# Loads of k and stores of the output with an outermost dimension of 32 or more rows, in a threshold-attention plus MLP kernel

## The chip, the cores and the metric

The kernel runs on one core of one Trainium2 chip. The metric is device time in microseconds (us), the median of several executions. Ratios use runs of the fast state alone; a median is taken over all runs of a kernel, and two of these (n2_order_only, v_late_weights) contain one slow run. The profile is one execution taken by the hardware profiler. PE is the TensorE matrix engine, DVE is VectorE, ACT is ScalarE, POOL is GpSimd, SP is SyncE, which here only issues DMAs. Times inside a profile count from the first instruction ("span").

## The reference

```python
# q, k, v: [8 batches, 8 heads, 576, 64] float32; tau = 0.02
scores = (q @ k.T) / 8
scores = where(scores >= max(scores, -1) - tau, scores, -1e9)
attn   = softmax(scores)                 # in each head
x      = (attn @ v), heads side by side  # [4608 tokens, 512]
h      = x @ w_in                        # w_in  [512, 2048]
out    = maximum(0.01 * h, h) @ w_out    # w_out [2048, 512], out [4608, 512] float32
```

## The kernel before

The program is built by a tile framework whose scheduler orders the instructions of each engine. It works in 160 steps: a step is one pair of heads and one chunk of 128 query rows (the fifth chunk has 64). A step computes scores on PE, takes their maximum on VectorE, exponentials on ScalarE, normalises on GpSimd, **turns the weights by a DMA transpose** (`wt<-w`), and five steps later (LAG) multiplies them with v on PE. Each batch's q and k are split into high and low fp16 parts and also turned by DMA transposes (`qst<-qs`, `kst<-ks`). Between these, PE works off units of the MLP; each 128 finished rows are stored.

All transposes, all q and k loads and all stores are issued from SP. v and the weights are loaded with a cast from GpSimd.

```python
    def load_qk(b, hb):                     # 4 heads: g = pair, h = head in the pair
        ...
        src_q = q[b, ds(4*hb, 4), :, :].rearrange("(g h) (p t) d -> h p g (t d)", h=2, t=9)
        src_k = k[b, ds(4*hb, 4), :, :].rearrange("(g h) (x p t) d -> x h p g (t d)", h=2, x=2, t=9)
        for g in range(2):
            for x in range(2):              # source [h=2, p=32, 576]: 64 rows of 2304 bytes
                nc.sync.dma_start(out=km[ds(64*x, 64), g, :], in_=src_k[x, :, :, g, :])
            if b == 0:
                nc.sync.dma_start(out=qm[:, g, :], in_=src_q[:, :, g, :])
        if b > 0:
            nc.sync.dma_start(out=qm[:, :, :], in_=src_q)
    ...
    def rows_of(b, c):                      # where 128 rows of the output go: [2, 64, 512]
        if c == 4:
            return out[ds(b*S, 2*S), :].rearrange("(b p t) d -> t b p d", t=9, b=2)[8]
        return out[ds(b*S, S), :].rearrange("(p t) d -> t p d", t=9)[ds(2*c, 2)]
    ...
            def fin():                      # the end of an MLP row block
                osb = sb.tile([128, 512], FP32, tag="osb", bufs=2, name="osb")
                nc.vector.tensor_copy(out=osb, in_=op)
                nc.sync.dma_start(out=G.stores[m], in_=osb)
    ...
            def evac():                     # attention output, PSUM -> x, fp16
                nc.scalar.activation(out=G.x[:, :, ds(col, n)], in_=pvp, func=AF.Copy, ...)
```

Of the kernel before, what the change touches and what calls it, by code (L numbers as in the profile page):

```python
# [12 lines left out]
AF = mybir.ActivationFunctionType  # L13
# [3 lines left out]
def kernel(  # L17
# [16 lines left out]
    nc = tc.nc  # L34
    B, H, S, D = q.shape
# [39 lines left out]
    def load_qk(b, hb):  # L75


        qm = sb.tile([128, 2, 576], FP32, tag="qm", bufs=2, name="qm")
        km = sb.tile([128, 2, 576], FP32, tag="km", bufs=2, name="km")
        src_q = q[b, ds(4 * hb, 4), :, :].rearrange("(g h) (p t) d -> h p g (t d)", h=2, t=9)  # L80
        src_k = k[b, ds(4 * hb, 4), :, :].rearrange("(g h) (x p t) d -> x h p g (t d)", h=2, x=2, t=9)
        for g in range(2):
            for x in range(2):
                nc.sync.dma_start(out=km[ds(64 * x, 64), g, :], in_=src_k[x, :, :, g, :])
            if b == 0:
                nc.sync.dma_start(out=qm[:, g, :], in_=src_q[:, :, g, :])
        if b > 0:
            nc.sync.dma_start(out=qm[:, :, :], in_=src_q)
        qms[b, hb], kms[b, hb] = qm, km

    def load_v(b):
# [106 lines left out]
    def h_unit(G, u):  # L198
        n = G.n
        per = 512 // n  # L200

        def mms():
            if u == 0:
                G.g = sb.tile([128, NJ, 256], FP16, tag="gT", bufs=2, name="gT")[:, :, 0:n]
            hp = ps.tile([128, per, n], FP32, tag="h", bufs=2, name="hp")
            for jj in range(per):
                j = u * per + jj
                for g in range(4):
                    nc.tensor.matmul(  # L209
                        out=hp[:, jj, :], lhsT=w_in16[:, g, ts(j, 128)], rhs=G.x[:, g, :],  # L210
                        start=(g == 0), stop=(g == 3), skip_group_check=True,
                    )

            def act():
                nc.scalar.activation(out=G.g[:, ds(u * per, per), :], in_=hp, func=AF.Relu, bias=0.0, scale=0.99)  # L215
                if (u + 1) * per == NJ:
                    for m in range(n // 128):
                        for c in range(4):
                            oq.append(lambda m=m, c=c: o_unit(G, m, c))
            return act  # L220
        return mms
# [47 lines left out]
    def rows_of(b, c):  # L269

        if c == 4:
            return out[ds(b * S, 2 * S), :].rearrange("(b p t) d -> t b p d", t=9, b=2)[8]
        return out[ds(b * S, S), :].rearrange("(p t) d -> t p d", t=9)[ds(2 * c, 2)]


    steps = []
# [9 lines left out]
    def group_of(b, c):  # L286

        if c == 4:
            key = ("t", b // 4)
            if key not in groups:  # L290
                t = b // 4
                groups[key] = Group(256, [rows_of(4 * t + 2 * m, 4) for m in range(2)])
            return groups[key], 64 * (b % 4), b % 4 == 3
        if b == B - 1 and c >= 2:
            if (b, c) not in groups:
                groups[b, c] = Group(128, [rows_of(b, c)])
            return groups[b, c], 0, True
        key = (b, c // 2, 0)
        if key not in groups:
            groups[key] = Group(256, [rows_of(b, 2 * (c // 2) + cc) for cc in range(2)])  # L300
        return groups[key], 128 * (c % 2), c % 2 == 1
# [41 lines left out]
    def pv(s):  # L343
        b, c, p = steps[s]
        wt = st[s]["wt"]
        vt = vts[b]
        n = 128 if c < 4 else 64
        if p == 0:
            pvt[0] = ps.tile([128, NP, n], FP32, tag="pv", bufs=1, name="pv")
        pvp = pvt[0]  # L350
        for j in range(5):
            for h in range(2):
                rhs = wt[:, 5 * h + j, :] if c < 4 else wt[:, j, ds(64 * h, 64)]
                nc.tensor.matmul(  # L354
                    out=pvp[ds(64 * h, 64), p, :], lhsT=vt[:, 2 * p + h, j, :], rhs=rhs,
                    start=(j == 0), stop=(j == 4), skip_group_check=True,
                    tile_position=(0, 64 * h),
                )
        if p == NP - 1:
            G, col, done = group_of(b, c)  # L360

            def evac():
                nc.scalar.activation(out=G.x[:, :, ds(col, n)], in_=pvp, func=AF.Copy, bias=0.0, scale=1.0)
                if done:
                    for u in range(NJ * G.n // 512):
                        hq.append(h_unit(G, u))
            return evac
        return None
# [30 lines left out]


    load_qk(0, 0)
    load_qk(0, 1)
    prep_q = deque()
    for p in range(NP):
# [9 lines left out]
    for g in range(4):  # L414
        nc.gpsimd.dma_start(
            out=w_out16[:, ds(4 * g, 4), :],
            in_=moe_w_out[ds(512 * g, 512), :].rearrange("(j p) d -> p j d", p=128))

    tick = {}
    for b in range(1, B):  # L420
        s0 = 20 * (b - 1)
        tick.setdefault(max(0, s0 - 4), []).append(lambda b=b: load_qk(b, 0))
        tick.setdefault(s0 + 12, []).append(lambda b=b: load_v(b))
        tick.setdefault(s0 + 4, []).append(lambda b=b: load_qk(b, 1))
        for p in range(NP):
            for i, t in enumerate(prep_tasks(b, p)):
                tick.setdefault(s0 + 1 + 4 * p + (i * 4) // 7, []).append(t)
# [7 lines left out]
    for s in range(NS + LAG + 1):  # L435
# [15 lines left out]
        if live:  # L451
            d = st[s]
# [19 lines left out]
        if live:  # L472
            nc.vector.scalar_tensor_tensor(  # L473
                out=d["W"][:, 0, 0:576], in0=s32, scalar=tb[:, 0:1], in1=E,
# [22 lines left out]
    while hq or oq:  # L497
        for q_ in (hq, oq):
            if q_:
                f = q_.popleft()()  # L500
# [37 lines left out]
```

## Time and profile before

| | before |
|---|---|
| median | 989.47 us (988.62 to 990.32, 2 runs) |
| PE busy, mean granted clock | 62%, 0.851 |
| first scores on PE | 55.9 us |
| step 10 starts its exp | 155.8 us |
| step 159 (the last) | 934.3 us |

The page first. The engine table (busy us, share of the span, number of instructions) and three rows of the 40 slices (tenths; PEclk is the granted PE clock, DMA the busy share of the 16 DMA engines), then the DMA queues:

```profile
PE 609.4 (62%) x4880; PEld 329.4 (33%) x4880; DVE 528.6 (54%) x1580; ACT 453.0 (46%) x894; POOL 440.1 (45%) x572
...
PEclk9999977777958876887679987888879998989998
DMA  3999989999979699998999999999996998849720
GB/s 82 101 139 89 129 158 178 114 140 128 145 90 142 97 117 96 136 139 116 126 100 138 116 140 104 113 126 130 127 144 79 150 136 118 120 78 115 102 60 33
...
q1 hardware_dynamic: 324768, 105.94, 87.3%
q0 software_dynamic: 23808, 8.92, 11.9%
```

No compute engine is full. DMA looks full, but moves little. What PE waits for (view of waits: who waited for whom, total us, times, longest us):

```profile
PE pv L354 <- DMA wt<-w: 124.3, 34, 10.3
PE sc L313 <- DMA qst<-qs: 109.3, 6, 55.9
PE sc L313 <- DVE s L377: 72.0, 28, 12.4
PE pv L354 <- ACT xT L363: 42.4, 15, 13.2
```

Two of the first three are transposes. The timeline shows one such case (start us, duration us, then, in brackets, the idle time before and what ended it). A pair of `qst` transposes occupies SP for 10.76 us and ScalarE stands 12.24 us for it; the next pair takes SP 3.57 us:

```profile
345.51 10.76 SPq L177 DMA_TRANSPOSE qst<-qs  x2
357.77 3.57 SPq L177 DMA_TRANSPOSE qst<-qs  x2
358.45 0.68 ACT L155 ACTIVATE qs<-qm 128x576 f16<-128x576 f32 x1 [12.24 <-DMA qst<-qs]
```

The trace also has every DMA packet: start, duration, size, queue. Sizes tell what a packet belongs to: 256 bytes on SP's queue are transposes, 2304 bytes are q and k rows, 2048 bytes are output rows. Counting them by the microsecond around that case (mean packets in flight, and packets completed):

```
us in span   transposes      q, k rows       output rows
             flight  done    flight  done    flight  done
  344          0.0      0      2.1     22      0.0      0     k load: 2 in flight
  347          0.0      0     16.6    147      0.0      0     q load: 16 in flight
  348          9.0    339      8.8     63      0.6      5
  349         20.0    112      0.2      2      1.9     21     a store begins: 2 in flight
  350 to 352  22.0      0      0.0      0      2.1     25     (each us) transposes stand
  353         22.0      0      0.3      3      1.8     22
  354         22.0      0      1.7     18      0.4      5     store ends, a k load begins
  356         20.3   1074      0.0      0      0.0      0     transposes run
```

Here is the whole case in eight lines (us 345 is like 344; 346 and 355, in which one state passes into the next, are left out). The store and the k load keep two packets in flight, as if only two of the 16 DMA engines worked. The transposes' packets are in flight all the while, so the DMA row shows 9 tenths, but not one completes for five microseconds; when the narrow transfers are over, a thousand complete in one.

### The profile page before, as it was taken

The numbers are of one execution on the slowest core, as the hardware profiler recorded it, in microseconds if no ns is written. First come the engines' busy times: TensorE is split into PE (matmuls) and PEld (weight loads), VectorE is DVE, ScalarE is ACT, GpSimd is POOL, SyncE is SP. The second block draws the span as 40 slices with busy tenths as digits, with TensorE's granted clock in tenths as the row PEclk, the third lists the DMA queues.
The fourth block names the chain that finished last, engine by engine and source line by source line (L and its number), as shares of the span: only waits on it lengthen the run. The fifth ranks groups of instructions, "written<-read, shape, count | busy, mean of one in ns | idle before, by whom it ended". The sixth has DMA issues, their size and how long they took to land. (4 is left out here: it accounts for less than half of the span.)

```text
span 987.9 us, 14544 instructions
## 1 busy us (share of the span) xinstructions
PE 609.4 (62%) x4880; PEld 329.4 (33%) x4880; DVE 528.6 (54%) x1580; ACT 453.0 (46%) x894; POOL 440.1 (45%) x572
## 2 busy tenths in 40 slices
PE   0010457466547634865549875766769688888995
PEld 0000122233314212442225442433335344555562
DVE  0040366564656514655438774754748576878800
ACT  2020345464544523545336573543647464765820
POOL 4250276264545533336534563625834563434500
PEclk9999977777958876887679987888879998989998
DMA  3999989999979699998999999999996998849720
GB/s 82 101 139 89 129 158 178 114 140 128 145 90 142 97 117 96 136 139 116 126 100 138 116 140 104 113 126 130 127 144 79 150 136 118 120 78 115 102 60 33
DMA packets 348651, 115.78 MB, mean 117 GB/s; under 512 B 333216, under 2 KB 335264, under 8 KB 348576
## 3 DMA queue, kind: packets, MB, share of 16 engines
q1 hardware_dynamic: 324768, 105.94, 87.3%
q0 software_dynamic: 23808, 8.92, 11.9%
q8 instruction: 38, 0.62, 0.3%
q14 instruction: 37, 0.30, 0.2%
HBM read 36.70 MB, written 9.44 MB: 47 GB/s over the span
## 5 line engine op out<-in xcount | busy, mean ns | idle before, releaser
L392 POOL TENSOR_SCALAR w<-w,rc 128x576 f16<-128x576 f16 x288 | 248.5, 873 | 290.9 <-DVE rc L390 280.7
L377 DVE TENSOR_SCALAR_CACHE_REDUCE s<-sc 128x576 f32<-128x576 f32 x288 | 213.6, 747 | 184.6 <-PE sc L319 178.5
L313 PE MATMUL sc<-kst,qst 128*128 128x288 f16 x512 | 121.1, 322 | 181.7 <-DMA qst<-qs 109.3
L473 DVE SCALAR_TENSOR_TENSOR w<-s,tb,E 128x576 f16<-128x576 f32 x160 | 148.5, 929 | 68.5 <-ACT E L459 59.3
L354 PE MATMUL pv<-wt,v 128*64 128x128 f16 (+1 forms) x1600 | 77.9, 238 | 167.3 <-DMA wt<-w 124.3
L209 PE MATMUL hp<-xT,win 128*128 128x256 f16 (+1 forms) x1216 | 173.2, 290 | 3.0 <-ACT gT L215 3.0
L231 PE MATMUL op<-wout,gT 128*128 128x512 f16 x576 | 164.4, 406 | 0.0
L459 ACT ACTIVATE E<-s,tb 128x576 f16<-128x576 f32 x160 | 122.1, 768 | 69.4 <-DVE tb L380 49.2
L354 PEld LDWEIGHTS <-v 128*64 128x64 f16 x1600 | 60.3, 122 | 195.3 <-issue 147.3
L209 PEld LDWEIGHTS <-win 128*128 128x128 f16 x1216 | 110.7, 104 | 43.2 <-issue 12.1
L313 PEld LDWEIGHTS <-qst 128*128 128x128 f16 x512 | 45.4, 104 | 231.4 <-DMA qst<-qs 112.2
L471 ACT ACTIVATE P<-s,tb 128x576 f16<-128x576 f32 x128 | 98.1, 766 | 49.4 <-DVE tb L380 42.9
L215 ACT ACTIVATE gT<-hp 128x512 f16<-128x512 f32 x144 | 83.4, 583 | 62.3 <-PE hp L209 52.4
L492 ACT ACTIVATE w<-P 128x576 f16<-128x576 f16 x128 | 86.7, 677 | 49.9 <-DVE P L491 30.9
L380 DVE SCALAR_TENSOR_TENSOR tb<-cm,mx,ca 128x2 f32<-128x2 f32 x288 | 99.3, 351 | 1.0
L155 ACT ACTIVATE qs<-qm 128x576 f16<-128x576 f32 x32 | 21.8, 682 | 149.2 <-DMA qst<-qs 141.9
L231 PEld LDWEIGHTS <-gT 128*128 128x128 f16 x576 | 58.7, 103 | 76.6 <-issue 28.7
L319 PE MATMUL sc<-kst,qst 64*128 64x288 f16 x512 | 83.4, 320 | 0.0
L112 ACT ACTIVATE ks<-km 128x256 f16<-128x256 f32 x64 | 23.8, 406 | 115.2 <-DMA kst<-ks 55.0
L226 PE MATMUL op<-wio,xT 128*128 128x512 f16 x144 | 59.3, 412 | 14.4 <-DVE osb L240 14.4
L163 POOL TENSOR_SCALAR qm<-qm 128x576 f32<-128x576 f32 x32 | 22.5, 702 | 97.9 <-ACT qs L155 93.7
L171 DVE COPY qs<-qs 128x576 f16<-128x576 f16 x32 | 15.4, 482 | 85.8 <-ACT qs L155 85.8
(37 smaller groups left out, 490.6 us busy)
## 6 DMA issues: line engine op xcount, KB each, us to landing
km<-in_k_dram SPq DMA_DIRECT2D x64, 144.0 KB
out_dram<-osb SPq DMA_DIRECT2D x36, 256.0 KB
qm<-in_q_dram SPq DMA_DIRECT2D x14, 576.0 KB
v<-in_v_dram POOLq DMA_DIRECT2D x32, 128.0 KB, 8.5
wt<-w SPq DMA_TRANSPOSE x160
win<-in_moe_w_in_dram POOLq DMA_DIRECT2D x4, 512.0 KB, 22.9
wout<-in_moe_w_out_dram POOLq DMA_DIRECT2D x4, 512.0 KB, 33.0
qm<-in_q_dram SPq DMA_DIRECT2D x4, 288.0 KB
```

The costliest lines, as they stand in the source:

```text
L209: nc.tensor.matmul(out=hp[:, jj, :], lhsT=w_in16[:, g, ts(j, 128)], rhs=G.x[:, g, :], start=(g == 0), stop=(g == 3), skip_group_check=True,)
L215: nc.scalar.activation(out=G.g[:, ds(u * per, per), :], in_=hp, func=AF.Relu, bias=0.0, scale=0.99)
L231: nc.tensor.matmul(out=G.op, lhsT=G.g[:, j, ds(128 * m, 128)], rhs=w_out16[:, j, :], start=False, stop=(j == NJ - 1), skip_group_check=True,)
L313: nc.tensor.matmul(out=sc[:, half, 0:288], lhsT=qa[1 - half], rhs=ka[half], start=True, stop=False, skip_group_check=True,)
L354: nc.tensor.matmul(out=pvp[ds(64 * h, 64), p, :], lhsT=vt[:, 2 * p + h, j, :], rhs=rhs, start=(j == 0), stop=(j == 4), skip_group_check=Tr ...
L377: nc.vector.tensor_scalar(out=halves(s32), in0=sc[:, :, 0:288], scalar1=C, scalar2=None, op0=AX.mult, op1=AX.max, accum_out=mx)
L380: nc.vector.scalar_tensor_tensor(out=tb, in0=cm[:, ds(2 * kind, 2)], scalar=mx, in1=ca[:, ds(2 * kind, 2)], op0=AX.mult, op1=AX.add)
L392: nc.gpsimd.tensor_scalar(out=W[:, h, 0:576], in0=W[:, h, 0:576], scalar1=rc[:, h : h + 1], scalar2=1.0, op0=AX.mult, op1=AX.mult,)
L459: nc.scalar.activation(out=E, in_=s32, func=AF.Exp, bias=tb[:, 1:2], scale=1.0)
L471: nc.scalar.activation(out=P, in_=s32b, func=AF.Identity, bias=tb2[:, 1:2], scale=KD)
L473: nc.vector.scalar_tensor_tensor(out=d["W"][:, 0, 0:576], in0=s32, scalar=tb[:, 0:1], in1=E, op0=AX.is_ge, op1=AX.mult, accum_out=d["sm"][ ...
L492: nc.scalar.activation(out=d["W"][:, 1, 0:576], in_=P, func=AF.Exp, bias=0.0, scale=1.0 / KD, accum_out=d["sm"][:, 1:2],)
```

## The change

Intent: give the DMA of k and of the output an outermost dimension that 16 divides, so that each spreads over 16 DMA engines. k is loaded in pieces of 32 rows of one head. For the output, rows 2c and 2c+1 of each of 64 groups become neighbours in the partition order, so the destination is [64, 2, 512]. To have the rows in that order, the copy of x out of PSUM now writes with a stride of two.

```diff
-        for g in range(2):
+        gs = [ds(0, 1), ds(1, 1)] if b == 0 else [ds(0, 2)]
+        for g in gs:
             for x in range(2):
-                nc.sync.dma_start(out=km[ds(64 * x, 64), g, :], in_=src_k[x, :, :, g, :])
-            if b == 0:
-                nc.sync.dma_start(out=qm[:, g, :], in_=src_q[:, :, g, :])
-        if b > 0:
-            nc.sync.dma_start(out=qm[:, :, :], in_=src_q)
+                for h in range(2):
+                    nc.sync.dma_start(out=km[ds(64 * x + 32 * h, 32), g, :], in_=src_k[x, h, :, g, :])
+            nc.sync.dma_start(out=qm[:, g, :], in_=src_q[:, :, g, :])
 ...
         if c == 4:
-            return out[ds(b * S, 2 * S), :].rearrange("(b p t) d -> t b p d", t=9, b=2)[8]
-        return out[ds(b * S, S), :].rearrange("(p t) d -> t p d", t=9)[ds(2 * c, 2)]
+            return out[ds(b * S, 2 * S), :].rearrange("(b p t) d -> t p b d", t=9, b=2)[8]
+        return out[ds(b * S, S), :].rearrange("(p t) d -> p t d", t=9)[:, ds(2 * c, 2), :]
 ...
-                nc.scalar.activation(out=G.x[:, :, ds(col, n)], in_=pvp, func=AF.Copy, bias=0.0, scale=1.0)
+                if c < 4:
+                    xo = G.x[:, :, ds(col, 128)].rearrange("f g (p i) -> f g i p", i=2)
+                    xi = pvp.rearrange("f g (i p) -> f g i p", i=2)
+                else:
+                    m, i = divmod(col // 64, 2)
+                    xo = G.x[:, :, ds(128 * m, 128)].rearrange("f g (p i) -> f g i p", i=2)[:, :, i, :]
+                    xi = pvp
+                nc.scalar.activation(out=xo, in_=xi, func=AF.Copy, bias=0.0, scale=1.0)
```

## The prediction

> **What bounds the kernel now.** No compute engine is full: the page's engine table has PE 62%, VectorE 54%, ScalarE 46%, GpSimd 45% of 987.9 us. The slices show the DMA engines near 9 tenths throughout, yet only 117 GB/s move. The trace's packet records explain it. 303,104 of 348,651 packets are the 256-byte packets of the on-chip transposes (w, q, k turned). Alone they complete at 735 per us; while k or q loads are in flight at 76, during output stores at 110, though about 18 stay outstanding. So a load or store freezes the transposes for as long as it lasts, and queued packets count as busy. It lasts long because a store (256 KB) keeps 2.2 packets in flight (84 ns each; one ran from 300.8 to 306 us), a k load 2.0. The Trainium skill, "DMA: Bandwidth & Descriptors", section "Why a DMA increments its semaphore by 16 and not by 1", says why: the engine count is the largest up to 16 that divides the outermost size of both sides; for k loads and stores that is 2. The q load, whose head and row dimensions merge into 128, shows 16 packets in flight: the trace agrees.
>
> By the records, k and q loads are in flight 276 us (q about 27), stores 203 us; for some 260 us of these transposes stand queued. PE's waits name it: 124 us for wt, 109 us for qst (mostly prologue: first scores at 55.9 us, next stall to 109.8). Steps (one exp each) take 3.4 to 3.6 us undisturbed, with gaps of 10 to 18 us; the average from 156 to 788 us is 5.3. The best 20 steps, without loads, take 66 us.
>
> **The change.** k: 32-row pieces, so 16 engines; 8 more issues, all in the first batch. Stores: outermost 64, so 16 engines. Bytes and packets stay. The output permutation moves into the PSUM copy of x (0.60 us, 40 times, now written with stride two; I expect no change). A store becomes 128 x 84 ns / 16 = 0.7 us (estimate), a pair of k loads about 0.8 us instead of 6. In flight: k 250 to about 35 us, stores 203 to about 30 us.
>
> **On the critical path.** Nearly all of the freezing: gaps of 10 us use up the five steps of slack (LAG). Estimates: step 10 starts at 95 us instead of 156; 150 steps at 4.0 us (PE's 609 us at mean clock 0.85 is 3.7 per step; fewer gaps should raise the clock) instead of 5.2; the tail of 48 us loses about 4 in the last store. 95 + 600 + 30 + 44: about 770 us, range 710 to 840. Chances: faster 0.97, same 0.02, slower 0.01.
>
> **What would show it.** Packets in flight during stores and k loads about 16; transposes near 700 packets per us throughout; PE's waits for wt and qst below 80 us together; mean DMA share clearly below 0.9; step gaps over 10 us rare; PE above 75%, granted clock above 0.9; first scores before 40 us.
>
> **What would make it wrong.** If transposes stall at each change between plain and transposing traffic, not for the transfer's length, the gain is smaller (850 or more). If the in-order chain of PE and GpSimd holds steps at 4.5 us, or the scheduler's new order hurts, 840. If the clock reaches 0.97 and steps 3.5 us, 700.

## The result, and the profile after

| | before | after |
|---|---|---|
| median | 989.47 us | 790.3 us (790.24 to 790.35, 2 runs) |
| ratio | 1 | 0.7987 (95%: 0.7953 to 0.8021) |
| PE busy, mean granted clock | 62%, 0.851 | 76%, 0.915 |
| first scores on PE | 55.9 us | 21.3 us |
| step 10 | 155.8 us | 98.9 us |
| step 159 | 934.3 us | 740.3 us |
| us per step between them | 5.22 | 4.30 |
| gaps of over 10 us between steps | 19 | 5 |

A ratio here and below is the mean time of one kernel's fast runs over the mean of the other's in the same rounds, so not quite the ratio of the medians. A second set of runs of the changed kernel on another chip (`r_after_again`, below) gave 792.38 us and 0.8003.

The same parts of the page after:

```profile
PE 598.0 (76%) x4880; PEld 325.1 (41%) x4880; DVE 530.1 (67%) x1580; ACT 455.5 (58%) x894; POOL 440.6 (56%) x572
...
PEclk9999997899998889897899889969997999899999
DMA  9999999999969988998689976899489956454501
GB/s 176 185 144 179 184 187 176 164 179 166 196 141 150 179 167 142 179 142 181 148 165 142 174 148 130 135 149 192 82 151 148 171 105 128 76 117 101 114 33 49
...
q1 hardware_dynamic: 326240, 105.95, 74.4%
q0 software_dynamic: 23808, 8.92, 10.4%
```

The bytes are the same. The busy time of every engine is the same to 2%. PE's waits:

```profile
PE sc L312 <- DMA qst<-qs: 60.4, 8, 21.3
PE sc L312 <- DVE s L384: 58.9, 47, 5.6
PE pv L353 <- ACT xT L370: 29.1, 18, 5.0
PE pv L353 <- DMA wt<-w: 22.8, 16, 3.8
```

PE's waits for `wt` fell from 124.3 to 22.8 us and for `qst` from 109.3 to 60.4. All of what is left for `qst` stands in the first 70 us. The stretch from step 10 to step 159 can be compared directly (view of windows: length, then busy us of PE, weight loads, VectorE, ScalarE and GpSimd, granted clock, DMA share, GB/s). Before, then after:

```profile
155.80:934.30 778.50, 534.82 (x4349) 292.84 (x4348) 481.11 (x1447) 402.14 (x789) 375.69 (x472) 0.83 1.03 121
```

```profile
98.90:740.30 641.40, 530.29 (x4397) 291.36 (x4396) 481.00 (x1447) 407.52 (x796) 377.11 (x476) 0.90 0.87 149
```

The work did not shrink: PE is busy 535 and 530 us in these stretches. What shrank is PE's idle time, from 244 to 111 us (length less busy time). What PE waited for most in this stretch, before, then after:

```profile
PE pv L354 <- DMA wt<-w: 112.4, 30, 10.3
PE sc L313 <- DVE s L377: 72.0, 28, 12.4
PE pv L354 <- ACT xT L363: 42.4, 15, 13.2
```

```profile
PE sc L312 <- DVE s L384: 47.5, 38, 5.6
PE pv L353 <- ACT xT L370: 29.1, 18, 5.0
PE pv L353 <- DMA wt<-w: 21.7, 15, 3.8
```

So 137 of the 199 us lie in this stretch (133 of PE's idle time, the rest of its busy time) and 57 before step 10; the end of the span after the last step gave some 5 (53.7 to 48.3 us; the last two stores together last 11.4 us before, the last one 0.8 us after). At the start not only transposes were late, but the loads themselves: the last packet of the first batch's q and k ended 34.8 us into the span before, and 15.8 us after.

The packet records after, counted as before:

| | before | after |
|---|---|---|
| transposes completed per us, nothing else in flight | 735 | 708 |
| the same while q or k loads are in flight | 76 | 532 |
| the same during stores | 110 | 662 |
| q and k loads in flight, us in all | 276 | 100 |
| stores in flight, us in all | 203 | 40 |
| a burst of 64 k rows, median | 4.3 us | 0.9 us |

(The rates count slices of 0.1 us in which over eight transpose packets are in flight. For the two middle rows such slices add up to 158 and 102 us before, and to 9 and 3 us after, so those rates after rest on little.) The mean number of packets in flight while a store runs is 10.8 (16 is the commonest), against 2.2. On SP, one store and the transpose behind it, a case from before, then one from after:

```profile
453.28 1.10 SPq L241 DMA_DIRECT2D out_dram<-osb  x1
454.44 4.92 SPq L177 DMA_TRANSPOSE qst<-qs  x1
```

```profile
256.40 0.59 SPq L240 DMA_DIRECT2D out_dram<-osb  x1
257.10 2.27 SPq L176 DMA_TRANSPOSE qst<-qs  x1
```

The loads from GpSimd's queue, which the change does not touch, also land sooner (page, last part: KB each, median us from issue to landing), before and after:

```profile
win<-in_moe_w_in_dram POOLq DMA_DIRECT2D x4, 512.0 KB, 22.9
wout<-in_moe_w_out_dram POOLq DMA_DIRECT2D x4, 512.0 KB, 33.0
```

```profile
win<-in_moe_w_in_dram POOLq DMA_DIRECT2D x4, 512.0 KB, 11.7
wout<-in_moe_w_out_dram POOLq DMA_DIRECT2D x4, 512.0 KB, 11.8
```

### The profile page after: what moved, and what is told of

The parts are those of the page before. It is cut to its first block, busy times and chain, and to the rows that moved or that the text cites. A ratio compares the mean times of both kernels' runs of the same rounds, so it can differ in the third digit from the quotient of the medians.

```text
span 788.6 us, 14565 instructions
## 1 busy us (share of the span) xinstructions
PE 598.0 (76%) x4880; PEld 325.1 (41%) x4880; DVE 530.1 (67%) x1580; ACT 455.5 (58%) x894; POOL 440.6 (56%) x572
## 3 DMA queue, kind: packets, MB, share of 16 engines
q1 hardware_dynamic: 326240, 105.95, 74.4%
q0 software_dynamic: 23808, 8.92, 10.4%
## 5 line engine op out<-in xcount | busy, mean ns | idle before, releaser
L399 POOL TENSOR_SCALAR w<-w,rc 128x576 f16<-128x576 f16 x288 | 245.7, 864 | 203.6 <-DVE rc L397 199.9
L312 PE MATMUL sc<-kst,qst 128*128 128x288 f16 x512 | 119.7, 318 | 119.9 <-DMA qst<-qs 60.4
L480 DVE SCALAR_TENSOR_TENSOR w<-s,tb,E 128x576 f16<-128x576 f32 x160 | 153.0, 958 | 40.0 <-ACT E L466 36.7
L208 PE MATMUL hp<-xT,win 128*128 128x256 f16 (+1 forms) x1216 | 167.2, 285 | 3.2 <-ACT gT L214 3.2
L230 PE MATMUL op<-wout,gT 128*128 128x512 f16 x576 | 159.5, 398 | 0.0
L208 PEld LDWEIGHTS <-win 128*128 128x128 f16 x1216 | 109.1, 103 | 38.4 <-issue 7.6
L353 PE MATMUL pv<-wt,v 128*64 128x128 f16 (+1 forms) x1600 | 76.4, 236 | 52.1 <-ACT xT L370 29.1
L318 PEld LDWEIGHTS <-qst 64*128 64x128 f16 x512 | 25.2, 94 | 72.0 <-issue 71.2
L126 POOL TENSOR_SCALAR km<-km 128x576 f32<-128x576 f32 x32 | 22.2, 693 | 56.6 <-ACT ks L117 56.4
L498 DVE TENSOR_SCALAR P<-P 128x576 int16<-128x576 int16 x128 | 48.3, 377 | 7.7 <-ACT P L478 7.4
```

What stands on the lines that cost most here:

```text
L208: nc.tensor.matmul(out=hp[:, jj, :], lhsT=w_in16[:, g, ts(j, 128)], rhs=G.x[:, g, :], start=(g == 0), stop=(g == 3), skip_group_check=True,)
L230: nc.tensor.matmul(out=G.op, lhsT=G.g[:, j, ds(128 * m, 128)], rhs=w_out16[:, j, :], start=False, stop=(j == NJ - 1), skip_group_check=True,)
L312: nc.tensor.matmul(out=sc[:, half, 0:288], lhsT=qa[1 - half], rhs=ka[half], start=True, stop=False, skip_group_check=True,)
L318: nc.tensor.matmul(out=sc[:, half, 0:288], lhsT=qa[half][r], rhs=ka[half][r], start=False, stop=True, skip_group_check=True, tile_position ...
L353: nc.tensor.matmul(out=pvp[ds(64 * h, 64), p, :], lhsT=vt[:, 2 * p + h, j, :], rhs=rhs, start=(j == 0), stop=(j == 4), skip_group_check=Tr ...
L399: nc.gpsimd.tensor_scalar(out=W[:, h, 0:576], in0=W[:, h, 0:576], scalar1=rc[:, h : h + 1], scalar2=1.0, op0=AX.mult, op1=AX.mult,)
```

## The experiments

Theory A: a transfer confined to two DMA engines holds up the transposes for as long as it lasts; the change makes it short. Rivals: B, the gain comes from the new order of instructions, which the scheduler changed on every engine; C, only the first loads of k matter; D, transposes stall at each change between plain and transposing traffic, whatever its length. All runs were compared with the kernel before on the same chip. n2_order_only, d4_store_on_4, x_plain_copy and n_no_loads compute wrong results; the others are correct.

| run | what | median us | ratio to before (95%) |
|---|---|---|---|
| n2_order_only | changed program, narrow k and stores | 977.1 | 0.9881 (0.9788 to 0.9974) |
| e1_k_wide | k wide, stores as before | 838.9 | 0.8500 (0.8454 to 0.8546) |
| e2_store_wide | stores wide, k as before | 927.96 | 0.9407 (0.9357 to 0.9458) |
| d4_store_on_4 | changed, stores on four engines | 823.69 | 0.8346 (0.8291 to 0.8401) |
| q_store_on_act | before, stores from ACT's queue | 1000.9 | 1.0177 (1.0111 to 1.0243) |
| x_plain_copy | changed, copy of x without stride | 789.5 | 0.8027 (0.7974 to 0.8080) |
| s_two_stores | changed, plain copy, two stores for one | 776.71 | 0.7884 (0.7822 to 0.7947) |
| v_late_weights | changed, weights loaded later | 767.29 | 0.7781 (0.7696 to 0.7866) |
| r_after_again | changed, again | 792.38 | 0.8003 (0.7954 to 0.8052) |
| n_no_loads | changed, q, k, v of first batches only | 758.99 | 0.7663 (0.7619 to 0.7707) |
| l_lag6 | changed, LAG 6 | 771.33 | 0.7803 (0.7772 to 0.7835) |
| b_both | late weights and two stores | 765.86 | 0.7734 (0.7691 to 0.7777) |

### n2_order_only: the new order with the old width

The source of each k load and the target of each store is a block of consecutive rows, viewed with an outermost 2. A comparison of the built programs shows the same instructions in the same order as in the changed kernel on all five engines (in the two traces one neighbouring pair on PE is swapped).

```diff
-   nc.sync.dma_start(out=km[ds(64*x + 32*h, 32), g, :], in_=src_k[x, h, :, g, :])
+   n = 64 if b else 32
+   nc.sync.dma_start(out=km[ds(64*x + 32*h, 32), g, :],
+                     in_=kr[ds(r0, n), :].rearrange("(a e) f -> e a f", e=2));  r0 += n
 ...
+   u = 32 + b // 2 if c == 4 else 4 * b + c
+   return out[ds(128*u, 128), :].rearrange("(a e) d -> e a d", e=2)
```

> The changed program with the same instructions in the same order on all five engines, but k loads and stores brought back to an outermost 2 (rows land permuted, so the result is wrong on purpose). Theory A (width: a transfer on two engines holds up the transposes for as long as it lasts): about as slow as before, 960 to 1010 us, 2 packets in flight during stores. Rival B (the gain comes from the scheduler's new instruction order and the regrouped loads of the first batch): near 790 to 850 us.

Measured: 977.1 us, with one of its four runs slow and left out of the ratio. Stores keep 2.0 packets in flight and transposes complete at 99 per us during them. PE waits:

```profile
PE sc L316 <- DMA qst<-qs: 94.0, 6, 58.9
PE pv L357 <- DMA wt<-w: 81.6, 31, 10.7
```

The order and the regrouped loads are worth 1.2% (95%: 0.3 to 2.1%). Rival B falls: of the 20%, almost all needs the width. Rival D, in the form stated, falls here too: this kernel issues as many plain transfers between the same transposes as the changed one, and takes 977 us against 790. The start is less clear: step 10 starts here at 135.8 us, 20 us earlier than before, so part of what is gained there may come with the order and the regrouped loads; its steps then take 5.25 us.

### e1_k_wide and e2_store_wide: the two halves alone

Each kernel takes one half of the diff and leaves the other as it was. By the traces, e1 has its instructions in the order of the changed kernel, and e2 in that of the kernel before. So e2 against before, and the changed kernel against e1, differ only in the stores and the copy of x that goes with them.

> Only the k loads changed, stores as before on two engines. Theory A: the k part of the queued time goes (158 of 260 us), so some 870 us (850 to 900); transposes still near 110 packets per us during stores. Rival C (only the prologue's k loads matter): about 930 us, and all of the gain before step 10.

> Only the stores changed (with the strided copy of x), k loads as before. Theory A: the store part goes (102 of 260 us), some 910 us (880 to 940), nothing gained before the first store near 300 us. Rival C: 985 us, as before.

Measured: 838.9 and 927.96 us. The two ratios multiply to 0.8500 x 0.9407 = 0.7996, which is the whole change. With k wide alone, step 10 starts at 98.5 us, as in the changed kernel, but steps after it take 4.57 us against 5.22, so rival C falls too: 57 us of e1's gain come before step 10 (up to 20 of them may be the new order's, see n2_order_only), and 97 us from the steps (778.5 less 681.2). Transposes still complete at only some 120 per us during e1's stores. With stores wide alone, step 10 stays at 154.7 us and the steps take 4.88. PE's waits, first e1, then e2:

```profile
PE sc L312 <- DMA qst<-qs: 59.9, 8, 21.5
PE pv L353 <- DMA wt<-w: 47.4, 19, 8.7
```

```profile
PE sc L313 <- DMA qst<-qs: 108.4, 6, 55.4
PE pv L354 <- DMA wt<-w: 100.8, 29, 8.8
```

I had expected 870 (850 to 900) and 910 (880 to 940), so e1 fell outside its range. The likely reason: I split the gain by the time that transposes stood queued (158 to 102 us) and forgot that at the start there are few transposes to queue, while ScalarE waits for k itself.

### d4_store_on_4: a middle width

The second half of the edit of n2_order_only on the changed kernel, with `e=4`.

> The changed kernel, same order of instructions, stores with an outermost 4 (rows land permuted, wrong on purpose). Theory A: a store lasts 128 x 84 ns / 4 = 2.7 us instead of 5.4, so about halfway or less between the stores on two engines (e1) and the changed kernel: 800 to 840 us. Rival D (a stall at each change between plain and transposing traffic, whatever its length): the same as the changed kernel or as e1, no grading with the width.

Measured: 823.69 us, between e1 (838.9) and the changed kernel (790.3). In flight during stores: 3.5 packets. A store lasts 6.3 us with two engines (median, in e1), 4.7 with four and 1.0 with sixteen, and the ratios follow: 0.850, 0.835, 0.799. The size of my estimate was wrong: a store on four engines took 4.7 us, not 2.7 (even after the transposes had ended, 4.3 us). Why it is not half of that on two engines is open; its rows lie at other addresses than in the other kernels. The grading by duration stands: the store's duration goes 30% of the way from 6.3 to 1.0 us, and the ratio 30% of the way from 0.8500 to 0.7987. During the stores transposes complete at about 250 per us, between the 110 and 662 of two and sixteen engines. This speaks against rival D once more.

### s_two_stores: twice the stores

The copy of x is written plainly again, and each block is stored as two transfers of [64, 512].

```diff
-                nc.sync.dma_start(out=G.stores[m], in_=osb)
+                for i in range(2):
+                    nc.sync.dma_start(out=G.stores[m][i], in_=osb[ds(64 * i, 64), :])
```

> A correct variant: plain copy of x as before, each store issued as two of 64 rows by 512, both with an outermost 64. Twice as many changes between plain and transposing traffic in the stores. Theory A: the same as the changed kernel within the scatter of the order, 780 to 800 us. Rival D (a stall per change): 36 more stalls, 820 us or more.

Measured: 776.71 us. Twice as many stores cost nothing. But the run does not test rival D as I meant it to: in 34 of the 36 pairs the second store's first packet starts before the first store's last has ended, so the number of changes between plain and transposing traffic hardly rose. What speaks against D is n2 and d4. The run is 1.3% faster by the ratios (0.7884 to 0.7987), which may be chance of order: this edit lets the scheduler reorder all engines.

### q_store_on_act: narrow stores from another queue

```diff
-                nc.sync.dma_start(out=G.stores[m], in_=osb)
+                nc.scalar.dma_start(out=G.stores[m], in_=osb)
```

> The kernel before, its narrow stores issued from ScalarE's queue instead of SyncE's, where the transposes are. If the hold-up is order within one queue (transposes stand behind a store's packets in the queue they share), transposes pass the store on the other queue, taking turns with it: well above 110 packets per us during stores (150 or more), and the time falls toward that of e2 (930 to 960 us). If it is the two busy engines themselves, whatever queue feeds them, the rate stays near 110 and the time within 1.5% of before.

Measured: 1000.9 us, 1.8% above before (95%: 1.1 to 2.4%). The rate fits the first expectation, the time neither (it is above the second's 1.5%). The rate of the transposes during stores rose to 174 per us from 110, as if the packets of the two queues took turns, but stores were in flight 235 us instead of 203 and the rate stayed far from 724 alone. The waits did not fall:

```profile
PE pv L354 <- DMA wt<-w: 175.6, 41, 17.6
PE sc L313 <- DMA qst<-qs: 105.2, 6, 55.4
```

So order within one queue seems to be part of the hold-up, but another queue for the stores alone did not help. That the two busy engines are the rest of it is likely, not shown. The Trainium skill, "DMA: Bandwidth & Descriptors", section "Issuing engines are not separate DMA queues", says that DMAs of all issuing engines run on the same 16 DMA engines; this run agrees, as far as a store on ACT's queue still held the transposes to 174 per us. Why the time rose rather than stayed is open: the 36 issues (median 522 ns each) now stand in ScalarE's stream, and the traces show that the order of the instructions changed on every engine.

### x_plain_copy: the strided copy

```diff
-                if c < 4: ...   # the strided views
+                xo, xi = G.x[:, :, ds(col, n)], pvp
                 nc.scalar.activation(out=xo, in_=xi, func=AF.Copy, bias=0.0, scale=1.0)
```

> The changed kernel with the PSUM copy of x written without the stride of two (rows land permuted, wrong on purpose), same order of instructions. The profile has the copy at 723 ns strided and 577 ns plain, 40 times; PE waits 29 us for it. If that lies on the critical path, 3 to 6 us (0.4 to 0.8%) faster than the changed kernel; if not, the same within 0.3%. It cannot explain more than 6 us of what the steps take above the predicted 4.0 us.

Measured: 789.5 us, 0.8027 against 0.7987 and 0.8003: the same. The copy's median is 577 ns here and in the kernel before, 723 ns in the changed kernel. The 40 copies take 26.9 us of ScalarE in the changed kernel and 21.6 here, and the difference of 5.3 us cost no measurable time.

### v_late_weights: the start

```diff
-    for g in range(4): <load w_in[g]>          # before the preparation of heads 4 to 7
-    for g in range(4): <load w_out[g]>         # after it
+    for g in range(4): tick[2 + g] <- load w_in[g], w_out[g]
-        tick[4 + g] <- wio_turn(g)             # first use of the weights
+        tick[6 + g] <- wio_turn(g)
-        rate = (1.12 if full else 0.56) if live else 2.0 ;  ... s >= 8
+        rate = (1.16 if full else 0.58) if live else 2.0 ;  ... s >= 10
```

> The changed kernel with the weight loads (8 of 512 KB) moved behind the first four heads' transposes, the MoE's start two steps later and its rate 1.16 for 1.12. In the changed kernel 8 waits of PE for qst, 60 us, all stand in the first 70 us, beside the weight loads. If the weight loads hold the transposes up there, step 10 starts near 75 us instead of 99 and the whole takes 765 to 780 us; if not, 790.

(MoE in this text is the MLP.) Measured: 767.29 us; one of the four runs was slow. Step 10 starts at 86.9 us instead of 98.9, not at 75; PE's wait for `qst` is 50.0 us instead of 60.4:

```profile
PE sc L312 <- DMA qst<-qs: 50.0, 8, 19.0
```

So the weight loads account for some 12 us of the start, and the larger part of these waits stays. Wide transfers may slow transposes as well: in the changed kernel, from 48 to 64 us, while weights are loaded, transposes complete at 167 per us, with 5.6 packets in flight on average, so that part of this may be that fewer were queued.

### r_after_again, n_no_loads, l_lag6: why a step takes 4.3 us

> The changed kernel again, as the yardstick on this chip for the three others: ratio to before 0.79 to 0.81, 780 to 800 us.

> The changed kernel without any load of q, k or v after the second batch's v: every batch uses the first one's q and k (wrong on purpose; the work of the engines and all transposes and stores stay). It asks why steps take 4.30 us and not the predicted 4.0. If what is left of the loads' hold-up is the cause, steps fall to 4.0 us or less and the time to 745 us or less. If it is the chain among PE, VectorE, ScalarE and GpSimd (PE busy 3.55 us a step, waits of PE for score buffers and the x copy), steps stay at 4.15 or more and the time at 765 to 785 us (the second batch's prologue loads gone).

> The changed kernel with one more step of slack between the scores and the product with v (LAG 6, one more buffer of w and of wt). PE's waits for wt, 22 us between 100 and 740 us, should go: 775 to 785 us if they are on the critical path, 790 if the other waits take their place.

The yardstick came out at 792.38 us. The edit of n_no_loads returns the first batch's tiles instead of loading, and scales them only once:

```diff
     def load_qk(b, hb):
+        if b > 0:
+            qms[b, hb], kms[b, hb] = qms[0, hb], kms[0, hb]
+            return
 ...  # load_v: returns its buffer for b > 1; the factors 64.0 become 64.0 if b == 0 else 1.0
```

Measured: 758.99 us and 4.07 us per step. That falls between my two thresholds. Against 4.27 us in the yardstick's trace and 4.30 in the first, the loads that are left seem to account for some 0.2 us of a step; this kernel's order of instructions differs as well, so the share of the loads is not shown.

LAG 6 (`LAG = 6`, `NW = 7`) gave 771.33 us and 4.16 us per step, 2.5% faster than the yardstick by the ratios, and better than the 775 to 785 us expected. PE's wait for `wt`, in the yardstick's trace, then here:

```profile
PE pv L353 <- DMA wt<-w: 26.6, 15, 5.4
```

```profile
PE pv L353 <- DMA wt<-w: 17.3, 18, 2.7
```

It did not go, and these 9 us are not the 21 us gained. What else the sixth step does is open; it too changed the order of the instructions.

### b_both: the best version

Late weights and two plain stores together.

> Late weights and two plain stores together (correct). If the two gains add: 767 x 776.7 / 790 = 754 us (745 to 765).

Measured: 765.86 us: 22.7% below before and 3.4% below the changed kernel on the same chip (0.7734 to 0.8003). It is the best correct kernel, but hardly better than late weights alone (0.7781, intervals overlap): the two gains did not add to the expected 754 us.

## Why the prediction was right

**The bound: right.** Transposes queued behind two-engine transfers (and, at the start, these transfers themselves), not any engine's work, made most of the lost time. The packet rates, the width runs (n2, e1, e2, d4) and the unchanged busy times show it. What is not shown is why some 20 packets of transposes stand while the narrow transfer has only two in flight.

**The rule of the width: right, with a miscount.** The Trainium skill, "DMA: Bandwidth & Descriptors", section "Why a DMA increments its semaphore by 16 and not by 1", lets the outermost size on both sides set the number of engines. The trace agrees: 2.2 packets in flight with 2, 3.5 with 4, 10.8 (a mean that includes the start and end of a short transfer) with 64. But 4 of the 36 stores were wide already: for c = 4 the kernel before stores [2, 64, 512] whose two outer dimensions have one common step and merge to 128. In its trace these four last 0.8 to 1.1 us, among others of 5.2 to 6.9 us. That is the cleanest comparison of all, inside one run, and I read past it. (The prediction's store "from 300.8 to 306 us" ran from 290.2 to 295.4 us of the span: packet records begin 10.5 us before the first instruction. Its average of 5.3 us a step from 156 to 788 us is a miscount too: 110 steps start there, 5.7 us each.)

**The start: right.** Step 10 was predicted at 95 us; it starts at 98.9. How much of the gain there is the width's is not settled, since n2_order_only with narrow loads reached 135.8.

**The steps: mis-sized.** Predicted 4.0 us, measured 4.30: 641 us for the stretch instead of 600. I expected the clock to shorten PE's work. The granted clock did rise (0.83 to 0.90 in that stretch), but PE's busy time fell only from 535 to 530 us. The Trainium skill, "TensorE: Matmul & The Clock Gate", section "What's actually happening", says that the clock is throttled by default and activity releases it; the clock records of these traces agree, with only 0.5 and 1.0 in them, and 133 us at 0.5 in that stretch after against 268 before, with PE waiting less. They also show why that saved little: of the half-clock time, PE stood idle for 121 us before and 20 after, and was busy for 148 and 113. So 100 of the 135 us that went were time in which PE waited anyway. PE's idle time of 0.75 us a step (111 us in 149 steps) then has no clock gain to set against it. By the waits in that stretch, 47.5 us of it are for score buffers that VectorE has yet to read, 29.1 for the copy of x, 21.7 for `wt`. Removing the remaining loads took off some 0.2 us a step, in another order of instructions; removing the stride of the copy took off nothing measurable; the rest of the 0.3 us is not settled. The loads also stayed in flight 100 us and the stores 40, not 62 and 30.

**The sum: a slip that helped.** 95 + 600 + 30 + 44 contains a 30 without a name; the 150 steps already reach the end of the work. Without it the prediction would have read about 740 us. The slip hid most of the step term's error of 41 us (the start was 4 us off, and the tail, 48.3 us instead of 44, another 4), and so the 770 looks better than its parts by luck.

**The copy of x: wrong, at no cost.** I expected no change; it takes 723 ns instead of 577.

**The signs:** first scores at 21.3 us (predicted below 40), 5 gaps over 10 us (19 before), PE 76%, clock 0.915: as predicted. Transposes complete at 708 per us alone and at 662 during stores, but at 532 during loads of q and k and at 167 beside the weight loads, so not near 700 throughout. Packets in flight during stores: 10.8 on average, not 16. Waits for `wt` and `qst` together 83.2 us, just above the 80 of the prediction. DMA share of the queues 74.4 + 10.4%, only a little below 0.9.

## What to carry to other kernels

Look at the outermost dimension of both sides of every DMA as it is after neighbouring dimensions have merged, and count packets in flight: two in flight went with an outermost size of two here. Here narrow transfers held up transposes that the critical path needed, and a DMA row at 9 tenths with 117 GB/s was the sign of it, since packets that waited counted as busy. A layout that makes the transfer wide removed most of that (two plain stores of 64 partitions did as well as one store with a permuted copy); issuing the narrow stores from another queue did not.

## What the Trainium skill lacked or had wrong

- "DMA: Bandwidth & Descriptors": it tells that a small outermost dimension confines a DMA to few engines, but not that such a DMA holds up the DMA transposes that run beside it. Here they fell from 735 packets completed per us to 76 to 110, and to none for five microseconds in the case shown.
- The same page, section "Why a DMA increments its semaphore by 16 and not by 1": its rule speaks of the pattern "as the instruction carries it"; it does not say that neighbouring dimensions of one common step are merged before that. A [2, 64, 512] store whose outer dimensions merge lasted 0.8 to 1.1 us, one whose do not, 5.2 to 6.9 us.
- The same page gives one bandwidth per engine and no measured time of a transfer on 4 engines; here it was 4.7 us for 256 KB against 6.3 on 2 and 1.0 on 16, so not in proportion.
- "SBUF — State Buffer", section "Door 1: The DMA port swizzle (why `[64,N]` ≈ `[32,N]`)", gives 8 bf16 elements as how far one can stride for free. ScalarE's copy of 128x512 from PSUM with fp16 written at a stride of two took 723 ns against 577 ns plain. The strided form also has one dimension more in its pattern; the runs do not separate the two, so the page may still be right.
- "Perfetto Trace Analysis", section "DMA Engine Tracks", says that slices "show actual busy time". The packet records of these profiles cannot be read so: a packet that stands counts as busy. In the case shown 22 transpose packets were in flight and none completed for five microseconds, and the DMA row was near 9 tenths while 117 GB/s moved.
